# Operands moved to other offsets in on-chip memory, and loads and cuts re-ordered, in a three-layer kernel

## The chip, the cores and the metric

One core of one Trainium2 chip runs the program. The metric is the device time of one execution in microseconds; the median of several runs counts. The profile is of one execution.

## The reference

Three layers follow each other, all in float32; no matrix may lose precision beyond that.

```python
scores = q @ k.T / sqrt(64) - log(448)        # 4 batches, 12 heads, 448 positions, 64 columns
x = sigmoid(scores) @ v                       # rearranged to 1792 tokens x 768
h = maximum(maximum(x @ w1, x @ w2), x @ w3)  # 768 x 768 each
y = h @ w_out1                                # 768 x 768
f = y @ w_in                                  # 768 x 2048
g = maximum(f, 0) + alpha * minimum(f, 0)
out = g @ w_out2                              # 2048 x 768
```

The weights arrive as float64; the kernel reads them as pairs of 32-bit words.

## The kernel before

**Numbers.** Each float32 operand is cut into a high part in float32r (ScalarE, `split_ops.hi`) and a rest (VectorE, `split_ops.lo`); a product is three matmuls, high x high, high x low, low x high (`three`, line 632). The matrices of the layers behind attention are multiplied by a seven-product scheme on 2 x 2 blocks (`unit_ops`, `form_ops`, `product`, `ff3`), so that sums and differences of blocks are made on VectorE before and after.

**Stages.** (1) Attention (line 369): 24 pairs of heads. `load_pair` brings q and k by eight DMAs of 32 partitions each, as runs of 32 floats, on SP's queue, two pairs ahead; `prep_ops` turns and cuts them; `scores` (line 494) makes a chunk of 128 keys at a time, ScalarE's sigmoid writes it into `a` tiles, `av` multiplies it with v. The first pair is loaded in rows and turned by TensorE against an identity (`first_pair`, line 398). (2) `product` (line 748): 9 units of the first weights, then, behind the `c` groups (line 817), 8 units of `w_in`; a unit is 14 products of 9 matmuls. (3) `c_group`: 24 groups of 18 matmuls, h times the fourth matrix. (4) `ff3` (line 937): 42 groups of 24 matmuls, g times the last matrix, with its operands stored to HBM and loaded again (`keep`, `load_g`, `load_w`).

**Order.** TensorE's order is written out by hand. The work of ScalarE ("A") and VectorE ("D"), loads ("L") and DMA issues ("Q") are `Op`s in two lists, `urgent` and `flow`; `advance` (line 168) is called after each piece of TensorE work with the columns that it took, gives both engines that much credit, and emits each op whose predecessors were emitted in an earlier step and whose gate is open. So an op's place in its engine's stream is set by the step in which it is emitted, and an instruction that waits holds all behind it on its engine. `load_half` (line 109) loads a half of a weight block on SP's queue into one of four `wr` buffers; `word_ops` (line 219) turns 64-bit words into float32 and asks for the half four places on. `unit_ops(0)` is started at pair 18 (line 595). `cut_h` for t = 2 and 3 is put into the list in the rounds (1, 1) and (2, 0) of the `c` stage (line 920).

**Memory.** Tiles lie in pools, on the left `const`, `wpool` and `slots_a` (later `slots_l`), on the right `edge`, `apool` (later `slots_c`, `slots_e`). A slot is 448 floats, 7 x 256 bytes, a weight slot 384 floats, 6 x 256 bytes. `bias_s` is 128 bytes wide, and `alpha_sb` and `nalpha` are 64 and 160, and with these every slot, weight slot and attention tile begins at a multiple of 256 bytes. In a matmul the moving operand (448 columns) is an `x`, `y`, `h` or `rf` slot, or q or `a` in attention; the stationary one (128 columns) is a weight slot or `lf`, or k or v. `swap` (line 1210) frees the pool c and opens e in its place, for the high and low parts of g; `turn_left` frees a and opens l.

Of the kernel before, what the change touches and what calls it, by code (L numbers as in the profile page):

```python
# [9 lines left out]
F32 = mybir.dt.float32  # L10
# [6 lines left out]
P = 128  # L17
# [4 lines left out]
def kernel(  # L22
# [43 lines left out]
    pools = {}  # L66
    room = {"a": 76, "c": 24, "e": 24, "l": 36}

    def slot(nm, pool="a", w=TW, dt=F32):
        return pools[pool].tile([P, w], dt, tag="s" + pool, name=nm, bufs=room[pool])  # L70

    def wslot(nm, dt=F32, pool="w"):

# [65 lines left out]
            self.lag = lag  # L139


    free = {"wr": 8, "wl": 4, "wk": 8, "ws": 5, "wf": 4, "rr": 14, "e": 8}
    urgent, flow = [], []
    STEP = 1700
    credit = {"A": 0, "D": 0}
# [73 lines left out]
    def word_ops(z, gate=None):  # L219


        st = {}

        def first():
            st["r"] = wraw.pop(z)
            st["T"] = wslot(f"wt{z}", U32)
            nc.scalar.activation(  # L227
                st["T"].bitcast(F32), st["r"][:, :, 1].bitcast(F32), AF.Abs, scale=2.0**-112
            )
            nc.scalar.activation(st["r"][:, :, 0], st["r"][:, :, 0], AF.Copy, scale=2.0**-29)  # L230

        def whole():
            nc.vector.tensor_scalar(st["T"], st["T"], 3, None, ALU.logical_shift_left)  # L233
            nc.vector.scalar_tensor_tensor(  # L234
                out=st["r"][:, :, 0],
                in0=st["r"][:, :, 1],
                scalar=0x80000000,
                in1=st["r"][:, :, 0],
                op0=ALU.bitwise_and,
                op1=ALU.bitwise_or,  # L240
            )
            nc.vector.tensor_tensor(out=st["T"], in0=st["r"][:, :, 0], in1=st["T"], op=ALU.add)  # L242
            word[z] = st["T"].bitcast(F32)
            load_half(z + 4)

        o = op(
            "A", 2 * HF, first,
            gate=lambda: z in since and tick[0] > since[z] + 3 and (gate is None or gate()),
        )
        return op("D", 3 * HF, whole, o)  # L250

    def split_ops(dst, make, src, w, *deps, seen=lambda x: x, put=lambda x: x, **kw):

# [115 lines left out]
    def attention(apool, ps_s, ps_v):  # L369
# [9 lines left out]
            for c in range(2)  # L379
            for p in (r, r + HK)  # L380
        ]
        raw, prepped, vts, at, pv = {}, {}, {}, {}, {}
# [4 lines left out]

        def load_first():

            kn, qn = (slot(x).rearrange("p (n d) -> p n d", d=32) for x in ("kn", "qn"))  # L390
            for t, src, queue in ((kn, k, nc.sync), (qn, q, nc.scalar)):
                queue.dma_start(
                    out=t.rearrange("p n d -> p (n d)"),
                    in_=src[0, :2].rearrange("j (p n) d -> (j p) (n d)", p=D),
                )
            raw[0] = (qn, kn)

        def first_pair():

            qn, kn = raw.pop(0)  # L400
            for which, t in (("k", kn), ("q", qn)):
                ps = ps_s.tile([P, 2, 512], F32, tag="sc", name=f"turn_{which}")[:, 0, :S]
                rows = t.rearrange("p n d -> p (n d)").rearrange("p (n d) -> p n d", d=D)
                for n in range(S // D):
                    for j in range(2):
                        nc.tensor.matmul(
                            ps[j * D : (j + 1) * D, n * D : (n + 1) * D],
                            rows[:, n],
                            ident[:, j * D : (j + 1) * D],
                            start=(n == 0),  # L410
                            stop=(n == S // D - 1),
                            skip_group_check=True,
                        )
                if which == "k":
                    hi, lo = (x[:, :S] for x in kk[0])
                else:
                    hi, lo = slot("qh0", dt=F32R), slot("ql0", dt=F32R)
                    prepped[0] = (hi, lo)

                seen = ps.rearrange("p (n r) -> p r n", r=D)  # L420
                hi, lo = (x.rearrange("p (r n) -> p r n", r=D) for x in (hi, lo))
                nc.scalar.copy(hi, seen)
                nc.vector.tensor_sub(lo, seen, hi.bitcast(F32))

        def load_v(i, queue):
            b, p = pairs[i]
            vt = apool.tile([P, 2, NCH + 1, D], F32, tag="vt", name=f"vt{i}", bufs=4)
            k0, h0, r0 = (KH, 0, KH) if i % 2 else (0, S - KH, 0)
# [65 lines left out]
        def scores(i, c, sc=None, stop=True):  # L494
# [10 lines left out]
            for z, (kx, qx) in enumerate(((kh, qh), (kl, qh), (kh, ql))):  # L505
# [80 lines left out]
        for i in range(0, n, 2):  # L586
            for z in range(2):
                if i + z + 2 < n:
                    load_pair(i + z + 2)
                if i + z == 8:  # L590
                    for h in range(4):
                        load_half(h)
                    with nc.allow_non_contiguous_dma(reason="a column of slopes per partition"):
                        nc.sync.dma_start(out=alpha_sb, in_=alpha.rearrange("(m p) -> p m", p=P))
                if i + z == 18:
                    unit_ops(0, zu[0])
                ops = prep_ops(i + z + 1)

# [62 lines left out]
    def ff(ps_m, dpool, swap, turn_left):  # L661
# [4 lines left out]
        def prelu(u, g, i, t, src, add=None):  # L666

            f, b = 2 * (u - ND0) + i, 2 * g + t
            s, o = {}, None
            if add is not None:  # L670
                o = op("D", TW, lambda: tensor_op(add, src, add, ALU.add), soon=True)

            def parts():
                x = src if add is None else add
                s["r"], s["n"] = slot(f"r{f}_{b}"), slot(f"n{f}_{b}")
# [15 lines left out]
            (p, o0), (r, o1) = slopes[u, g, 0, 0], slopes[u, g, 1, 1]  # L691

            def sum1():
                s["t"] = slot(f"t1_{u}_{g}")
                tensor_op(s["t"], s["r"], p["r"], ALU.subtract)

            def sum3():
# [8 lines left out]
        def keep(u, g, what, src, o):  # L706
            kp = u - ND0

            def store():
                x = fd[what, g, kp] = dpool.tile(  # L710
                    [P, TW], F32, tag=f"g{len(fd)}", name=f"gd{what[0]}{what[1]}_{g}_{kp}"
                )
                nc.gpsimd.dma_start(out=x, in_=src())  # L713

            stored.append(op("Q", 0, store, o))

        def evict(u, g, i, t, src, other=None):

# [186 lines left out]
        for n, (g, r) in enumerate(quads):  # L905
# [10 lines left out]
            for i in range(2):  # L916
                if g == 0 and r < HK - 1 and i == 0:
                    for h in range(4):
                        conv_ops(NB + 4 * (r + 1) + h)
                if g == 0 and (r, i) in ((1, 1), (2, 0)):  # L920
                    for m in range(KDM - 2):
                        cut_h(m, 1 + r, far[m, 1 + r])
                for t in range(2):
                    c_group(r + HK * i, 2 * g + t)
                    if (n, i, t) == (0, 0, 0):
# [4 lines left out]
            (0, 1), (0, 0), (2, 1), (3, 1), (2, 0), (4, 1), (1, 1), (3, 0), (5, 1), (6, 1),  # L930
        ))
        swap()
        for k in seq[3:]:
            step(ND1 - 1, k, 0)
        run[0](stored)

    def ff3(ps_m, dpool, fd, wd, slopes, seq, turn_left):

# [8 lines left out]
        def load_op(homes, make, src, gate, lag):  # L947
# [3 lines left out]
            def home():  # L951
                return [
                    h for h in homes
                    if free[h] > 0
                    and (h in ("wr", "ws", "wf", "e") or "l" in pools)
                    and (h != "wf" or len(pair) == KP // 2 and free["wr"] == KP)
                ]

# [47 lines left out]
        def left_ops(k, kp):  # L1006
# [183 lines left out]

        return run
# [72 lines left out]
```

## Time and profile before

| | |
|---|---|
| median of 3 runs | 877.12 us |
| lowest, highest | 876.55, 886.61 us |
| the profiled execution | 877.7 us |
| its span, first to last instruction | 875.6 us |
| TensorE (PE) busy | 867.1 us |
| weight loads (PEld) | 747.8 us |
| VectorE (DVE) | 676.2 us |
| ScalarE (ACT) | 527.8 us |

Times of the rows are microseconds from the span's start unless marked ns. PE is the matmul, PEld the weight load that runs beside it; SPq, ACTq and POOLq are DMA issues by those engines. A matmul's own duration in a row includes its way through the array, so that one starts before its predecessor ends: the pace is read from starts. What stands behind `<-` at a row's end is what ended the idle time before it.

### The profile page before, as it was taken

Reading aid. Unit: us, or ns where it says so; the run is one execution under the profiler, and the core shown is the slowest. Engines: PE = TensorE matmul, PEld = TensorE weight load, DVE = VectorE, ACT = ScalarE, POOL = GpSimd, SP = SyncE. Lnnn points to the kernel's source line nnn. Section 1 sums busy time; section 2 is a strip of 40 time slices with the busy share of each in tenths; the row PEclk is TensorE's granted clock in tenths of the full one; section 3 lists DMA queues with packets and bytes.
Section 4 is the critical chain, followed back from the end, with each engine's and each line's share of the span. In section 5 each row is a group of like instructions: output and inputs, shape, how many; then the busy total and the mean of one; then the engine's idle time right before and its main releaser. Section 6 shows DMA issues by size and latency. Waiting matters only on the chain.

```text
span 875.6 us, 13589 instructions
## 1 busy us (share of the span) xinstructions
PE 867.1 (99%) x4604; PEld 747.8 (85%) x4604; DVE 676.2 (77%) x1323; ACT 527.8 (60%) x1034; POOL 146.5 (17%) x249
## 2 busy tenths in 40 slices
PE   9999999999999999999999999999999999999997
PEld 4555557999999999999899999999998999999997
DVE  5888895888889878787687877777766778768851
ACT  5888896755655554666566767667664755443430
POOL 4333320002111201200000122122211011001211
PEclk9999999999999999999999999999999999999999
DMA  8887570547675655632112443354426999445412
GB/s 159 149 181 142 107 170 1 153 127 231 208 203 159 223 146 170 216 91 73 36 53 99 135 148 134 137 178 167 154 97 209 371 335 373 164 151 159 136 49 64
DMA packets 180501, 137.00 MB, mean 156 GB/s; under 512 B 100576, under 2 KB 170336, under 8 KB 180432
## 3 DMA queue, kind: packets, MB, share of 16 engines
q1 hardware_dynamic: 163536, 93.25, 38.5%
q0 software_dynamic: 13952, 42.09, 13.2%
q10 hardware_dynamic: 2944, 0.80, 0.4%
q8 instruction: 36, 0.59, 0.3%
q14 instruction: 33, 0.27, 0.1%
HBM read 102.28 MB, written 33.82 MB: 155 GB/s over the span
## 4 chain that ended last, share of the span: by engine, by line
PE 96%; DVE 1%; ACT 1%; issue 1%; DMA 0%; SPq 0%; DVEq 0%; ACTq 0%
PE u_1X L652 14%; PE u_0X L652 14%; PE eW L652 10%; PE c L652 10%; PE eX L652 10%; PE pav L529 7%; PE u_1W L652 7%; PE u_0W L652 7%; PE sc L508 7%; PE u_1V L652 4%; PE eV L652 3%; PE u_0V L652 3%; DMA kr<-in_k_dram 0%; PE warm L580 0%; ACT r L676 0%
## 5 line engine op out<-in xcount | busy, mean ns | idle before, releaser
L519 ACT ACTIVATE a<-sc,bias_s 128x896 f32<-128x896 f32 x84 | 82.2, 1015 | 13.8 <-PE sc L508 13.8
L529 PE MATMUL pav<-a,vt 128*64 128x448 f32 (+1 forms) x384 | 70.3, 551 | 0.0
L227 ACT ACTIVATE wt<-wr 128x384 f32<-128x384 f32 x112 | 62.1, 555 | 12.4 <-DMA wr<-in_moe_w_dram 5.4
L242 DVE CUSTOM_DVE_ANT_0 wt<-wr,wt 128x768 uint16<-128x768 uint16 x112 | 62.6, 559 | 3.9
L234 DVE SCALAR_TENSOR_TENSOR wr<-wr 128x384 uint32<-128x384 uint32 x112 | 62.0, 554 | 0.9
L230 ACT ACTIVATE wr<-wr 128x384 uint32<-128x384 uint32 x112 | 61.9, 552 | 0.0
L680 DVE SCALAR_TENSOR_TENSOR r<-n,nalpha,r 128x448 f32<-128x448 f32 x64 | 43.3, 683 | 22.4 <-ACT n L677 22.3
L713 POOL DMA_DIRECT2D gd<-r x48 | 26.0, 541 | 201.0 <-DVE r L680 199.2
L529 PEld LDWEIGHTS pav<-a,vt 128*64 128x64 f32 (+1 forms) x384 | 21.0, 135 | 38.5 <-issue 36.8
L430 POOL DMA_DIRECT2D vt<-in_v_dram x46 | 35.3, 769 | 64.0 <-PE pav L529 63.6
L871 POOL DMA_DIRECT2D wd<-wt x32 | 17.5, 546 | 169.5 <-DVE wt L242 149.6
L1108 POOL DMA_DIRECT2D out_dram<-o x28 | 17.6, 635 | 168.3 <-DVE o L1103 168.3
L233 DVE TENSOR_SCALAR wt<-wt 128x384 uint32<-128x384 uint32 x112 | 39.8, 355 | 5.6 <-ACT wt L227 5.6
L508 PE MATMUL sc<-qh,kh 64*128 64x448 f32 x192 | 38.1, 393 | 1.7 <-DVE qh L482 0.9
L780 ACT COPY u<-u_1X 128x448 f32<-128x448 f32 x34 | 18.1, 533 | 33.0 <-PE u_1X L652 33.0
L508 PE MATMUL sc<-ql,kh 64*128 64x448 f32 x192 | 35.4, 365 | 0.0
L508 PEld LDWEIGHTS sc<-qh,kh 64*128 64x128 f32 x192 | 18.0, 184 | 20.2 <-ACT a L519 7.8
L508 PE MATMUL sc<-qh,kl 64*128 64x448 f32 x192 | 35.0, 361 | 0.0
L832 ACT COPY y<-c 128x448 f32<-128x448 f32 x24 | 12.8, 533 | 34.1 <-PE c L652 34.0
L780 ACT COPY u<-u_0X 128x448 f32<-128x448 f32 x34 | 18.1, 534 | 25.0 <-PE u_0X L652 24.4
L276 DVE TENSOR_TENSOR u<-u_0W,u 128x448 f32<-128x448 f32 x28 | 17.4, 623 | 19.3 <-ACT u L780 18.7
L767 ACT COPY u_0V<-u_0X 128x448 f32<-128x448 f32 x17 | 8.8, 518 | 32.7 <-PE u_0X L652 32.7
(836 smaller groups left out, 2882.1 us busy)
## 6 DMA issues: line engine op xcount, KB each, us to landing
gl<-gd SPq DMA_DIRECT2D x79, 224.0 KB, 4.4
wr<-in_moe_w_out_dram SPq DMA_DIRECT2D x44, 384.0 KB, 4.2
wr<-in_moe_w_dram SPq DMA_DIRECT2D x36, 384.0 KB, 3.8
wr<-in_moe_w_in_dram SPq DMA_DIRECT2D x32, 384.0 KB, 3.8
wl<-wd SPq DMA_DIRECT2D x64, 192.0 KB, 4.1
gd<-r POOLq DMA_DIRECT2D x48, 224.0 KB, 2.2
gl_T<-gdT SPq DMA_DIRECT2D x32, 224.0 KB, 5.1
wd<-wt POOLq DMA_DIRECT2D x32, 192.0 KB, 4.0
```

The lines of the kernel that those rows point to most:

```text
L227: nc.scalar.activation(st["T"].bitcast(F32), st["r"][:, :, 1].bitcast(F32), AF.Abs, scale=2.0**-112)
L230: nc.scalar.activation(st["r"][:, :, 0], st["r"][:, :, 0], AF.Copy, scale=2.0**-29)
L233: nc.vector.tensor_scalar(st["T"], st["T"], 3, None, ALU.logical_shift_left)
L234: nc.vector.scalar_tensor_tensor(out=st["r"][:, :, 0], in0=st["r"][:, :, 1], scalar=0x80000000, in1=st["r"][:, :, 0], op0=ALU.bitwise_and, ...
L242: nc.vector.tensor_tensor(out=st["T"], in0=st["r"][:, :, 0], in1=st["T"], op=ALU.add)
L430: queue.dma_start(out=vt[:, j, :NCH], in_=v[b, 2 * p + j, k0 : k0 + NCH * P].rearrange("(c p) d -> p c d", p=P),)
L508: nc.tensor.matmul(sc[:, j, :S], kx[r, c0 : c0 + P], qx[r], start=(start and z == 0), stop=(stop and z == 2),)
L519: nc.scalar.activation(a, sc[:, :, :S], AF.Sigmoid, bias=bias_s, scale=scale)
L529: nc.tensor.matmul(pv[i][j * D : (j + 1) * D, :S], vts[i][r, j, c, :], a[r, j, :], start=start, stop=stop,)
L652: nc.tensor.matmul(ps[:, : rh.shape[-1]], lt, rh, start=(start and z == 0), stop=(stop and z == len(mms) - 1), skip_group_check=True,)
L680: nc.vector.scalar_tensor_tensor(out=s["r"], in0=s["n"], scalar=nalpha[:, f : f + 1], in1=s["r"], op0=ALU.mult, op1=ALU.add,)
L780: nc.scalar.copy(side[g, k], banks[X][:, :TW])
```

## The change

Pads of 48 floats (192 bytes) are put in front of the slots of a and, in l, behind the tag `lf`; pads of 16 floats (64 bytes) stand behind the slots in the pools on the right, whose slots begin 64 bytes lower by that. So moving operands of these pools begin 192 bytes behind a multiple of 256; stationary ones in `wpool`, `apool` and `lf` begin at 0. The first pair's q and k share one attention tile; q is turned first, and k's first 128 columns are turned and cut on their own, with positions left in the order that the turn gives, and v of that pair is loaded to match. The first eight halves of weights ask for the next half in an op of their own; `unit_ops(0)` starts at pair 14; `cut_h` for t = 2 and 3 goes into rounds (1, 0) and (1, 1). Behind `swap` stands one more `advance`; the seven `gl` loads of the last layer's first operand go into `a` slots before `swap` instead of `e` slots behind it; two late results go into `e` slots, which are given back when they are stored; the last operand is put into the list after product 5 instead of at `plan`.

```diff
+    def pad(pool, w):
+        if pool not in padded:
+            padded.add(pool)
+            pools[pool].tile([P, w], F32, tag="pad", name=f"pad_{pool}")
+
     def slot(nm, pool="a", w=TW, dt=F32):
-        return pools[pool].tile([P, w], dt, tag="s" + pool, name=nm, bufs=room[pool])
+        if pool == "a":
+            pad(pool, 48)
+        t = pools[pool].tile([P, w], dt, tag="s" + pool, name=nm, bufs=room[pool])
+        if pool != "a":
+            pad(pool, 16)
+        return t
...
-    free = {"wr": 8, "wl": 4, "wk": 8, "ws": 5, "wf": 4, "rr": 14, "e": 8}
+    free = {"wr": 8, "wl": 4, "wk": 8, "ws": 5, "wf": 4, "rr": 14, "e": 4, "a": 7}
...
-            load_half(z + 4)
+            if z >= 8:
+                load_half(z + 4)
...
-        return op("D", 3 * HF, whole, o)
+        o = op("D", 3 * HF, whole, o)
+        if z < 8:
+            op("Q", 0, lambda: load_half(z + 4), o, lag=1)
+        return o
...
-            kn, qn = (slot(x).rearrange("p (n d) -> p n d", d=32) for x in ("kn", "qn"))
+            t = apool.tile([P, 2, S], F32, tag="a", name="kqn", bufs=2 * NCH + 1)
+            kn, qn = (t[:, x].rearrange("p (n d) -> p n d", d=32) for x in range(2))
...
+            for t, ps, n0, n1 in ((qn, ps_q, 0, S // D), (kn, ps_k0, 0, 2), (kn, ps_k, 2, S // D)):
...
+            nc.scalar.copy(qh, seen)
+            nc.vector.tensor_copy(first_k[0], ps_k0)
+            nc.vector.tensor_sub(first_k[1], ps_k0, first_k[0].bitcast(F32))
+            nc.vector.tensor_sub(ql, seen, qh.bitcast(F32))
+            nc.scalar.copy(kh, ps_k)
+            nc.vector.tensor_sub(kl, ps_k, kh.bitcast(F32))
...
+            if i == 0:
+                n = S // D
+                for j in range(2):
+                    rows = v[b, 2 * p + j].rearrange("(r n) d -> r n d", n=n)
+                    for x in range(2):
+                        queue.dma_start(out=vt[x * D : (x + 1) * D, j, :NCH], in_=rows[:, x : n - 1 : 2])
+                queue.dma_start(
+                    out=vt[:KH, :, NCH],
+                    in_=v[b, 2 * p : 2 * p + 2].rearrange("j (r n) d -> r j n d", n=n)[:, :, n - 1],
+                )
...
+            if (i, c) == (0, 0):
+                kh, kl = first_k
+                three = ((kh, qh), (kl, qh), (kh, ql))
+            elif i == 0:
+                three = ((kh, qh), (kh, ql), (kl, qh))
...
-                if i + z == 18:
+                if i + z == 14:
                     unit_ops(0, zu[0])
...
+            home = lambda: "e" if (u, i, t) == (ND1 - 1, 0, 1) and "e" in pools else "a"
...
+            if u == ND1 - 1 and what in ("T1", "T3"):
+                o.ends.append({"h": "e"})
...
-                if g == 0 and (r, i) in ((1, 1), (2, 0)):
+                if g == 0 and (r, i) in ((1, 0), (1, 1)):
                     for m in range(KDM - 2):
-                        cut_h(m, 1 + r, far[m, 1 + r])
+                        cut_h(m, 2 + i, far[m, 2 + i])
...
         swap()
+        advance(STEP)
         for k in seq[3:]:
             step(ND1 - 1, k, 0)
-        run[0](stored)
+            if k == 5:
+                run[0][0]()
+        run[0][1](stored)
...
+                    and (h != "a" or (U, seq[2], 1) in made)
...
-                ("rr", "e") if n else ("e",),
-                lambda h: slot(nm, "e") if h == "e" else tile_l("rr", nm, TW, 14),
-                lambda: fd[key], lambda: ("l" if n else "e") in pools and key in fd,
-                8 if n else 1 if kp < 3 else 2,
+                ("rr", "e") if n else ("a",),
+                lambda h: tile_l("rr", nm, TW, 14) if h == "rr" else slot(nm, h),
+                lambda: fd[key], lambda: (not n or "l" in pools) and key in fd,
+                8 if n else 1,
...
+                if (k, kp, x) == (1, 0, "h"):
+                    return lf[k, kp][x]
...
-                return ((U, seq[kp - 4], 0) if kp > 3 else (U - 1, 6, 1)) in made
+                return ((U, seq[kp - 3], 0) if kp > 3 else (U - 1, 6, 1)) in made
...
+        def last_right():
+            right_ops(0, KP - 1, soon=True)
+
         def plan():
-            right_ops(0, KP - 1, soon=True)
...
+                        lf[1, 0]["h"] = tile_l("lf", "lf1_0h", HF, 2 * KP, F32R)
+                        pad("l", 48)
```

## Rows read from the trace of the kernel before

**Rows 1.** The page: busy us (share of the span) and instructions of each engine.

```profile
PE 867.1 (99%) x4604; PEld 747.8 (85%) x4604; DVE 676.2 (77%) x1323; ACT 527.8 (60%) x1034; POOL 146.5 (17%) x249
```

**Rows 2.** Stretches: us, busy PE, PEld, DVE, ACT, POOL (instructions), PE clock, DMA share, GB/s.

```profile
100.00:150.00 50.00, 48.98 (x327) 28.59 (x324) 40.22 (x81) 40.78 (x67) 9.09 (x13) 1.00 0.37 84
300.00:350.00 50.00, 50.00 (x249) 46.36 (x248) 39.95 (x82) 26.37 (x57) 6.49 (x12) 1.00 0.57 170
850.00:876.00 26.00, 21.06 (x104) 19.18 (x103) 3.25 (x5) 0.00 (x0) 2.50 (x4) 0.98 0.23 54
```

**Rows 3.** Pieces of the chain that ended last: start, us, engine, tile, instructions.

```profile
375.28 44.65 PE c L652 x216
...
486.18 3.65 PE u_1X L652 x18
...
725.14 58.37 PE eW L652 x288
```

**Rows 4.** Middle of a unit, timeline of PE and PEld; its weight loads in the groups.

```profile
300.05 0.37 PE L652 MATMUL u_1V<-x_1h,f_1l 128*128 128x448 f32 x1
300.05 0.19 PEld L652 LDWEIGHTS u_1V<-x_1l,f_1h 128*128 128x128 f32 x1
...
300.25 0.36 PE L652 MATMUL u_1V<-x_1l,f_1h 128*128 128x448 f32 x1
...
L652 PEld LDWEIGHTS u_0V<-x_1h,f_1h 128*128 128x128 f32 x27 | 5.1, 188 | 0.4
```

**Rows 5.** Attention: timeline of two paired loads of pav; the loads of sc in the groups.

```profile
52.27 0.14 PEld L529 LDWEIGHTS pav<-a,vt 128*64 128x64 f32 x2 [0.23 <-issue]
52.64 0.14 PEld L529 LDWEIGHTS pav<-a,vt 128*64 128x64 f32 x2 [0.23 <-issue]
...
L508 PEld LDWEIGHTS sc<-qh,kh 64*128 64x128 f32 x192 | 18.0, 184 | 20.2 <-ACT a L519 7.8 <-issue 4.2 <-ACT x_4h L256 2.8
```

**Rows 6.** The first 8 us, timeline of all engines.

```profile
1.27 0.96 ACTq L430 DMA_DIRECT2D vt<-in_v_dram  x2
...
4.06 1.21 PE L406 MATMUL turn_k<-ident,kn 128*64 128x64 f32 x28
...
5.09 1.00 PE L406 MATMUL turn_q<-ident,qn 128*64 128x64 f32 x28
5.31 0.53 ACT L422 CAST kh<-turn_k 128x448 fp32r<-128x448 f32 x1 [2.61 <-PE turn_k L406]
...
6.69 0.62 DVE L423 TENSOR_TENSOR ql<-turn_q,qh 128x448 fp32r<-128x448 f32 x1 [0.19 <-ACT qh L422]
6.71 0.47 PE L508 MATMUL sc<-qh,kh 64*128 64x448 f32 x2 [0.62 <-ACT qh L422]
...
7.68 0.36 PE L508 MATMUL sc<-qh,kh 64*128 64x448 f32 x2
```

**Rows 7.** End of attention, timelines of SP's queue, DVE and PE.

```profile
110.12 0.39 SPq L115 DMA_DIRECT2D wr<-in_moe_w_dram  x1
...
121.97 0.65 DVE L466 STREAM_TRANSPOSE kt<-kr 128x448 f32<-128x448 f32 x1 [1.02 <-DMA kr<-in_k_dram]
...
126.80 0.47 PE L508 MATMUL sc<-qh,kh 64*128 64x448 f32 x2 [0.91 <-DVE qh L482]
```

**Rows 8.** Two stretches of PE (us, PE busy, clock, DMA); SP's queue; a wait at 640:675.

```profile
419.74:423.99 4.25, 4.06 (x19) 1.00 0.00 0
664.76:671.47 6.71, 5.97 (x25) 1.00 0.42 153
...
644.90 19.37 SPq L963 DMA_DIRECT2D gl<-gd  x9
...
PEld eX L652 <- DVE rf_0l L260: 0.6, 1, 0.6
```

**Rows 9.** Attention's middle, a stretch as in rows 2; the page's loads of k.

```profile
50.00:100.00 50.00, 50.00 (x370) 27.72 (x368) 39.83 (x78) 41.04 (x57) 20.82 (x30) 1.00 0.81 156
...
kr<-in_k_dram SPq DMA_DIRECT2D x92, 56.0 KB, 2.6
```

More of the change, by code (lines that the diff above doesn't have):

```diff
@@ L67 @@
     room = {"a": 76, "c": 24, "e": 24, "l": 36}
-    def slot(nm, pool="a", w=TW, dt=F32):
-        return pools[pool].tile([P, w], dt, tag="s" + pool, name=nm, bufs=room[pool])
+    padded = set()
+    def pad(pool, w):
+        if pool not in padded:
+            padded.add(pool)
+            pools[pool].tile([P, w], F32, tag="pad", name=f"pad_{pool}")
+    def slot(nm, pool="a", w=TW, dt=F32):
+        if pool == "a":
[4 more added lines that the diff above has]
+        return t
     def wslot(nm, dt=F32, pool="w"):
@@ L381, in attention @@
         ]
-        raw, prepped, vts, at, pv = {}, {}, {}, {}, {}
+        raw, prepped, vts, at, pv, first_k = {}, {}, {}, {}, {}, []
         kk = [
@@ L400, in first_pair @@
             qn, kn = raw.pop(0)
-            for which, t in (("k", kn), ("q", qn)):
-                ps = ps_s.tile([P, 2, 512], F32, tag="sc", name=f"turn_{which}")[:, 0, :S]
+            ps_q = ps_s.tile([P, 2, 512], F32, tag="sc", name="turn_q")[:, 0, :S]
+            ps_k0 = ps_v.tile([P, 512], F32, tag="pv", name="turn_k0")[:, :P]
+            ps_k = ps_s.tile([P, 2, 512], F32, tag="sc", name="turn_k")[:, 0, : S - P]
+            for t, ps, n0, n1 in ((qn, ps_q, 0, S // D), (kn, ps_k0, 0, 2), (kn, ps_k, 2, S // D)):
@@ L403, in first_pair @@
                 rows = t.rearrange("p n d -> p (n d)").rearrange("p (n d) -> p n d", d=D)
-                for n in range(S // D):
+                for n in range(n0, n1):
                     for j in range(2):
                         nc.tensor.matmul(
-                            ps[j * D : (j + 1) * D, n * D : (n + 1) * D],
+                            ps[j * D : (j + 1) * D, (n - n0) * D : (n - n0 + 1) * D],
                             rows[:, n],
                             ident[:, j * D : (j + 1) * D],
-                            start=(n == 0),
-                            stop=(n == S // D - 1),
+                            start=(n == n0),
+                            stop=(n == n1 - 1),
@@ L412, in first_pair @@
                             skip_group_check=True,
                         )
[L414 to L423, printed above, removed]
+            prepped[0] = slot("qh0", dt=F32R), slot("ql0", dt=F32R)
@@ new lines, in first_pair @@
+            seen = ps_q.rearrange("p (n r) -> p r n", r=D)
+            qh, ql = (x.rearrange("p (r n) -> p r n", r=D) for x in prepped[0])
+            kh, kl = (x[:, P:S] for x in kk[0])
+            first_k.extend(slot(f"k{x}00", dt=F32R)[:, :P] for x in "hl")
+            nc.scalar.copy(qh, seen)
[3 more added lines that the diff above has]
+            nc.scalar.copy(kh, ps_k)
@@ L427, in load_v @@
             vt = apool.tile([P, 2, NCH + 1, D], F32, tag="vt", name=f"vt{i}", bufs=4)
+            if i == 0:
[8 more added lines that the diff above has]
+                )
+                vts[i] = vt
+                return
             k0, h0, r0 = (KH, 0, KH) if i % 2 else (0, S - KH, 0)
@@ L504, in scores @@
                 sc = ps_s.tile([P, 2, 512], F32, tag="sc", name=f"sc{i}_{c}")
-            for z, (kx, qx) in enumerate(((kh, qh), (kl, qh), (kh, ql))):
+            three = ((kh, qh), (kl, qh), (kh, ql))
+            if (i, c) == (0, 0):
+                kh, kl = first_k
+                three = ((kh, qh), (kl, qh), (kh, ql))
+            elif i == 0:
+                three = ((kh, qh), (kh, ql), (kl, qh))
+            for z, (kx, qx) in enumerate(three):
                 for j in range(2):
@@ L674, in parts @@
                 x = src if add is None else add
-                s["r"], s["n"] = slot(f"r{f}_{b}"), slot(f"n{f}_{b}")
+                s["r"], s["n"] = slot(f"r{f}_{b}", home()), slot(f"n{f}_{b}")
                 nc.scalar.activation(s["r"], x, AF.Relu)
@@ L693, in sum1 @@
             def sum1():
-                s["t"] = slot(f"t1_{u}_{g}")
+                s["t"] = slot(f"t1_{u}_{g}", home())
                 tensor_op(s["t"], s["r"], p["r"], ALU.subtract)
@@ L713, in store @@
                 nc.gpsimd.dma_start(out=x, in_=src())
-            stored.append(op("Q", 0, store, o))
+            o = op("Q", 0, store, o)
+            stored.append(o)
+            if u == ND1 - 1 and what in ("T1", "T3"):
+                o.ends.append({"h": "e"})
         def evict(u, g, i, t, src, other=None):
@@ L954, in home @@
                     if free[h] > 0
-                    and (h in ("wr", "ws", "wf", "e") or "l" in pools)
+                    and (h in ("wr", "ws", "wf", "e", "a") or "l" in pools)
+                    and (h != "a" or (U, seq[2], 1) in made)
                     and (h != "wf" or len(pair) == KP // 2 and free["wr"] == KP)
@@ L1189, in run @@
             drain()
-        return run
+        return last_right, run
     with tc.manual_schedule():
```

## The prediction

> **What bounds the kernel now.** I read the busy shares first, then PE by stretches, then the chain in order of time, because an engine that is busy for 99% of the span [rows 1] can still be run at a poor pace, and only starts of single instructions tell that. The reader is to see two things. First, PE is hardly ever idle: in the middle of the run whole stretches of 50 us show 50.00 us of PE, and what is missing lies in few places, 1.02 us where attention ends and some 5 us behind the last matmul [rows 2]. So edits that move loads and cuts about can win only the little that is missing. Second, the pace: the chain's pieces give 58.37 us for 288 matmuls, 202.7 ns each, in the last product, and 202.8 ns in the middle one; one stretch, the `c` groups, runs at 44.65/216 = 206.7 ns [rows 3]. The granted clock there is 1.00, the 2.4 GHz level [rows 2], so it isn't the clock.
>
> What sets 202.7 ns? A weight load starts as its predecessor's matmul starts (both at 300.05) and takes 188 ns; the next matmul starts at 300.25 [rows 4]. So load plus some 12 to 15 ns of handing over is the whole period. Where the loaded block is half as wide (`pav`, 64 columns), the load takes 0.14 us and the parallel pair of matmuls follows at 0.377 us, 188.5 ns a matmul [rows 5]: there the load ends long before the stream does, and the period is shorter by 14 ns a matmul. I read this as: outside attention the period is the chain of weight loads, not the stream of the moving operand.
>
> The Trainium skill (TensorE: Matmul & The Clock Gate, Back-to-back issue gap) puts the isolated gap at N/2.4 + 2.5 ns, an estimate of 189 ns for 448 columns; the rows show 202.7, so the rule's term is not the one that binds here. By the rule 14 ns a matmul would be there to win; by the row they are won only if the load gets shorter.
>
> **The change part by part.** The sum is made against the profiled execution's own 877.7 us (875.6 of span and 2.1 around it), 0.6 above the 877.12 median of the runs shown.
>
> *The pads.* They issue no instruction. They move the moving operands of all 3,582 full-width matmuls (17 units x 14 products x 9, 24 `c` groups x 18, 42 `e` groups x 24) from 0 to 192 bytes behind a multiple of 256; stationary operands stay at 0, but for the `c` weights that live in `a` slots. No matmul of the trace has another offset, so their price isn't shown, and I bound it. Below: every matmul falls to the 188.5 ns of `pav` [rows 5], 14.2 x 3,582 = -50.9 us. Above: every matmul goes at the `c` stretch's 206.7 ns [rows 3], 4.0 x 3,582 = +14.3 us. I take 0, nearest to the reading that the loads of stationary blocks, which do not move, are the chain: the load takes 188 ns wherever its matmul's operand lies.
>
> *The first pair* (`first_pair`, `load_v`). Before: k is turned from 4.06, q from 5.09, `kh` is cut at 5.31, `qh` after it, and the first score starts at 6.71, the second chunk at 7.68, held up by `ql` (6.69 to 7.31) [rows 6]. After: q is turned first, so `qh` is cut at 5.31; the 8 + 20 records of k follow, and the first 128 columns are cut on DVE by 5.9, so `sc` starts behind the turns, at 6.1. `ql` ends near 6.6 instead of 7.31, the rest of k is cut on ACT by 6.7, and the second chunk starts at about 6.8: 0.9 us earlier, of which I take 0.8 (next late is the sigmoid, which sets the score banks free). The two more loads of v on ACT's queue take half a microsecond each, by the 0.96 us of two, from 1.27 [rows 6]; `qh` waits until 5.31 in any case, so they are hidden; without that cover they would cost 1.0. Bounds: 0 and -1.0.
>
> *Weights earlier* (`unit_ops(0)` at pair 14, `load_half` as an op of its own one step later). Before, SP stands at a weight load until DVE has emptied its buffer (110.12), and k and q of the next pairs queue behind; DVE then waits for `kr` (1.02 us before 121.97) and PE for `qh` (0.91 us before 126.80) [rows 7]. Four such loads now meet four earlier pairs, each queued a step later on SP. A wait is still behind each, so I take half of the 1.02 us [rows 2], -0.5; bounds -1.0 and +1.0 (it happens once more).
>
> *The `c` stage* (`cut_h` for t = 2, 3 half a round earlier). The group at 419.74 takes 4.25 us for 18 matmuls, 18 x 0.2067 = 3.72 at its own pace, so its wait for the late cuts of h costs 0.5 [rows 8]. The cuts go to steps with free ACT and DVE: -0.5; bounds -0.5 and 0. The pace of 206.7 ends at this wait; without it, it could last longer, and that is a rival below.
>
> *The last product's start* (gl loads into `a` slots before `swap`, one more `advance`, `last_right` after k = 5, T1 and T3 into `e`). SP takes 19.37 us over nine `gl` issues, since the `e` slots they want are still read under their old name. The first group has 24 matmuls in 6.71 us, against 24 x 0.2027 = 4.86: 1.85 us lost in four waits like that for `rf_0l` [rows 8]. Seven loads now have a home of their own; 14 cuts and the last one fit into the four products in front. I take -1.8; bounds -1.85 and 0. What is late next would be the slots of the later `gl`, which start with 4 `e` homes in place of 8 and get four back with the T stores.
>
> Sum: -0.8 - 0.5 - 0.5 - 1.8 = -3.6, so 874.1 for an execution like the profiled one, and 873.5 on the scale of the median.
>
> **The rivals.**
>
> *A: the pace falls.* If the moving stream and the weight load, which start together [rows 4], hinder each other by both beginning at 0, the shift frees some of the 14.2 ns. Half of it is 7.1 x 3,582 = 25 us: 848. For it: load and stream do start within a hundredth of a microsecond, and half-width loads show the shorter period. Against it: the load's 188 ns are the same in every group, and 184 ns for the half-height blocks of `sc` [rows 5].
>
> *B: the pace rises,* by the pads or because no wait ends the 206.7 ns phase any more: 873.5 + 14.3 = 888. For it: that phase follows no operand and lasts 54 us. Against it: the pieces before and after it are at 202.7 [rows 3].
>
> *C: attention becomes bound by DMA (the other side).* The transposing loads bring rows of 32 floats, 128 bytes, which at 0 never cross a multiple of 256 and at 192 cross every second time. 92 such loads of 56 KB each for k, as many for q; the DMA engines are at 0.81 already [rows 9]. If a crossing row costs a second piece, k and q cost up to 1.5 times; at a share of 0.81 x 1.5 = 1.22 the 110 us of attention stretch by 24: 898. It decides once the loads grow by 1/0.81 = 1.23. Against it: k and q are not all of the 0.81.
>
> The Trainium skill (DMA: Bandwidth & Descriptors, How a descriptor splits into AXI transactions) speaks for C: a piece must begin at a 256-byte boundary, and one that doesn't start there is split and pays for the bytes in front. No row here shows a load at another offset.
>
> *D: the edits don't do what they say:* waits move to the next late load, at the end of attention or among the later `gl` (the DMA share is high there too), and what the start wins they lose: 877.
>
> **How the numbers follow.** Forecast 0.55, with a range of its own of 870 to 877; A 0.22; B 0.11; C 0.06; D 0.06. The range reaches down to the middle of A, 848, which leaves out half of it (0.11), and up to B's 890, which leaves out C and a little of B (0.08). Two per cent, about what a measurement of this kernel can tell from no change, is 17.5 us: faster is below 859.6, which takes nine tenths of A, 0.20. Slower is above 894.7: C and 0.02 of B, 0.08. The rest, 0.72, is within.
>
> **What would show it.** Right: the chain's pieces after still at 202 to 203 ns a matmul, loads at 188; `sc` starting near 6.1; 100 to 150 with PE near 49.5; the first `eX` group in 4.9 us. Wrong: a period that has moved by more than 2 ns in `u` or `e`, with the load's start or length moved with it (A, B); PE waiting for `qh` or `kr` over and over between 20 and 110, with the DMA share at 1 (C). The forecast as a whole is wrong if the period per matmul is not 202.7.

## The result, and the profile after

The changed kernel takes 872.04 us (median; 871.82 to 872.61), 0.9897 of the kernel before, with a 95% interval of [0.9866, 0.9928]. In that comparison the kernel before spread from 876.55 to 886.61 with a median of 880.38, which flatters the ratio. A later comparison gave 872.53 against 877.23, 0.9946 [0.993, 0.9961], a ratio that leaves out one execution of the kernel before at 4441.93 us; I take that one, 4.7 us. Both lie within 2%. The profiled execution took 872.05 us, with a span of 870.2; it is 5.65 us shorter than the one profiled before, 0.95 more than the 4.7.

The page's busy shares and the stretches of the kernel after (columns as in [rows 1] and [rows 2]):

```profile
PE 862.4 (99%) x4604; PEld 746.3 (86%) x4604; DVE 677.4 (78%) x1325; ACT 527.4 (61%) x1034; POOL 146.6 (17%) x249
```

```profile
10.00:20.00 10.00, 8.65 (x66) 4.78 (x64) 6.33 (x12) 6.88 (x9) 5.50 (x9) 1.00 0.92 169
...
50.00:100.00 50.00, 49.89 (x366) 27.03 (x363) 42.90 (x85) 44.22 (x66) 20.26 (x29) 1.00 0.84 165
100.00:150.00 50.00, 50.00 (x338) 30.05 (x335) 41.40 (x83) 40.44 (x63) 9.76 (x14) 1.00 0.47 83
300.00:350.00 50.00, 50.00 (x249) 46.36 (x248) 38.98 (x81) 25.38 (x55) 7.00 (x13) 1.00 0.60 172
...
661.60:668.50 6.90, 6.90 (x36) 6.40 (x35) 6.78 (x13) 5.10 (x11) 2.29 (x5) 1.00 0.74 224
```

The holes of [rows 2] and [rows 8] are closed: 100 to 150 has 50.00 us of PE (48.98 before), and the last product's first 6.90 us hold no gap. A new hole stands at the start: 8.65 of 10 us between 10 and 20.

Pieces of the chain that ended last (start, us, engine, tile, instructions), to be held against [rows 3]:

```profile
374.03 83.77 PE c L695 x414
...
661.64 29.12 PE eX L695 x144
...
719.88 58.24 PE eW L695 x288
```

A last-product matmul takes 58.24/288 = 202.2 ns (202.7 before), one of the `c` stage 83.77/414 = 202.3. The 206.7 ns stretch of before is gone. All `c` groups but the first form one piece: no wait divides them any more.

The same place in a unit as [rows 4] on the timeline, and its loads in the groups:

```profile
300.30 0.37 PE L695 MATMUL u_1V<-x_1h,f_1l 128*128 128x448 f32 x1
...
300.30 0.19 PEld L695 LDWEIGHTS u_1V<-x_1l,f_1h 128*128 128x128 f32 x1
...
300.51 0.36 PE L695 MATMUL u_1V<-x_1l,f_1h 128*128 128x448 f32 x1
```

```profile
L695 PEld LDWEIGHTS u_0V<-x_1h,f_1h 128*128 128x128 f32 x27 | 5.1, 187 | 0.5
```

Load and matmul still start together. The mean of all 3,582 recorded loads of a full block went from 187.9 to 187.5 ns, by nearly as much as the period. So these two traces alone don't tell a shorter load from a shorter gap behind it; `e3` below does, with loads of 187.5 ns too and a period of 200.0.

The start of the kernel after, and three marks further on, from the timeline:

```profile
1.21 3.64 SPq L486 DMA_DIRECT2D kr<-in_k_dram  x4
1.26 1.38 ACTq L458 DMA_DIRECT2D vt<-in_v_dram  x2
...
4.41 1.03 PE L430 MATMUL turn_q<-ident,kqn 128*64 128x64 f32 x28 [0.44 <-DMA kqn<-in_q_dram]
...
5.30 2.15 SPq L486 DMA_DIRECT2D qr<-in_q_dram  x4
6.22 0.47 PE L551 MATMUL sc<-qh,kh 64*128 64x448 f32 x2
7.22 0.37 PE L551 MATMUL sc<-qh,kh 64*128 64x448 f32 x2
...
15.90 0.47 PE L551 MATMUL sc<-qh,kh 64*128 64x448 f32 x2 [1.35 <-DVE qh L519]
...
140.64 0.47 PE L695 MATMUL u_0X<-x_0h,f_0l 128*128 128x448 f32 x1
...
865.12 0.36 PE L695 MATMUL eW<-rf_7h,lf_7h 128*128 128x448 f32 x1
```

The same marks of the kernel before (k's and q's loads of the second pair; the third pair's first scores; first `u`; last matmul):

```profile
1.21 3.04 SPq L449 DMA_DIRECT2D kr<-in_k_dram  x4
4.29 2.05 SPq L449 DMA_DIRECT2D qr<-in_q_dram  x4
...
15.03 0.47 PE L508 MATMUL sc<-qh,kh 64*128 64x448 f32 x2
...
141.26 0.47 PE L652 MATMUL u_0X<-x_0h,f_0l 128*128 128x448 f32 x1
...
870.70 0.37 PE L652 MATMUL eW<-rf_7h,lf_7h 128*128 128x448 f32 x1
```

How early the first scores come depends on the clock too. While `turn_q` and `turn_k` run, pairs of matmuls start 107 ns apart until the trace's record of the granted clock begins, at 1.00, and 58 ns apart from then on. It begins at 4.49 before and at 4.39 here, so the two starts can be set against each other to some 0.2 us. In the runs below it begins anywhere between 4.35 and 9.89; the time ahead of it has no record, and prints as 1.00.

The ledger by these marks and by `eX` (664.76 before [rows 8], 661.64 after):

| stretch | change, us | of it |
|---|---|---|
| to the first scores | -0.5 | 6.71 to 6.22 |
| first scores to third pair's | +1.4 | 8.32 to 9.68 |
| on to the first `u` | -1.5 | 126.23 to 124.74; the waits of [rows 7] gone |
| `u` and `c` stages | -2.5 | pads 0.45 ns x 2,574 = 1.2; the `c` wait 0.5; the 206.7 stretch some 1 |
| last product | -2.5 | the waits of [rows 8] 1.85; pads 0.45 ns x 1,008 = 0.5 |

Together -5.6, the difference of 870.70 and 865.12 in the two profiled executions. The rest of this document separates pads from re-ordering and finds what sets 202.2.

### The profile page after: what moved, and what is told of

Read it like the earlier page. It is cut to its first block, busy times and chain, and to the rows that moved or that the text cites. A ratio compares the mean times of both kernels' runs of the same rounds, so it can differ in the third digit from the quotient of the medians.

```text
span 870.2 us, 13603 instructions
## 1 busy us (share of the span) xinstructions
PE 862.4 (99%) x4604; PEld 746.3 (86%) x4604; DVE 677.4 (78%) x1325; ACT 527.4 (61%) x1034; POOL 146.6 (17%) x249
## 4 chain that ended last, share of the span: by engine, by line
PE 98%; DMA 1%; SPq 1%; DVE 0%; issue 0%; DVEq 0%
PE u_0X L695 14%; PE u_1X L695 14%; PE c L695 10%; PE eW L695 10%; PE eX L695 10%; PE pav L572 8%; PE u_0W L695 7%; PE u_1W L695 7%; PE sc L551 7%; PE u_0V L695 4%; PE u_1V L695 4%; PE eV L695 3%; SPq L486 1%; DMA kr<-in_k_dram 0%; DMA qr<-in_q_dram 0%
```

## The experiments

The kernels before of these comparisons had medians of 876.93 (`e1` to `e4`), 877.28 (`e5` to `e8`) and 877.23 (`f1` to `f4`). Each diff is against the changed kernel unless it says otherwise. "Difference" is the start of the moving operand less that of the stationary one, modulo 256 bytes.

**Re-ordering alone** (`e1_no_pads`): difference 0.

```diff
     def pad(pool, w):
-        if pool not in padded:
-            padded.add(pool)
-            pools[pool].tile([P, w], F32, tag="pad", name=f"pad_{pool}")
+        return
```

> The changed kernel without its pads: every operand begins at 0 behind a multiple of 256 again, all else as changed. Theory P (the offset between moving and stationary operands decides whether the chain of weight loads can fall into the 206.7 ns pace, and the pads hold it off): the pace outside attention is 202.7 ns at best, 0.45 above the 202.2 of the changed kernel, which is 3,582 x 0.45 = 1.6 us, and some stretches at 206.7 come back: 874 to 880 us, with several us between the runs. Rival S (the pace of 206.7 came from the waits that the re-ordering took away, the pads do nothing but the 0.45): 873.6 us, runs within 1 us, no stretch at 206.7.

Measured: 873.39 (873.01 to 873.88), 0.9962 [0.995, 0.9975]. Its chain:

```profile
720.86 58.37 PE eW L693 x288
```

Its timeline: q's loads of the second pair, the first and the third pair's scores, the first `u`:

```profile
5.16 1.96 SPq L484 DMA_DIRECT2D qr<-in_q_dram  x4
6.83 0.47 PE L549 MATMUL sc<-qh,kh 64*128 64x448 f32 x2
...
15.44 0.47 PE L549 MATMUL sc<-qh,kh 64*128 64x448 f32 x2 [0.27 <-DVE qh L517]
...
140.41 0.47 PE L693 MATMUL u_0X<-x_0h,f_0l 128*128 128x448 f32 x1
```

Its stretch from 50 to 100:

```profile
50.00:100.00 50.00, 49.89 (x366) 27.13 (x364) 42.93 (x86) 44.24 (x66) 20.57 (x29) 1.00 0.77 159
```

That is what rival S expected, 873.6 and no stretch at 206.7. The pace is 58.37/288 = 202.7, as before. All re-ordering together is worth 876.93 - 873.39 = 3.5 us. SP's second batch goes out at 5.16, not 4.29: that push belongs to the re-ordering, not to the pads. The first scores are at 6.83 and not at 6.22 because the clock's record begins at 6.25 here. The third pair's scores still wait 0.27 us for q, so their 15.44 is set by the loads. The same stretch of attention has a DMA share of 0.77 with rows at 0 and 0.84 with rows at 192; but the kernel before has 0.81 at 0, and the second run of the change (`f1`) 0.80 at 192, so the difference isn't clear of what changes from one execution to the next.

**Pads alone** (`e2_pads_only`): the kernel before with `pad`, its two calls in `slot` (48 for a, 16 for the others) and the one behind `lf`. Of the diff against the kernel before, the part in `slot`:

```diff
...
-        return pools[pool].tile([P, w], dt, tag="s" + pool, name=nm, bufs=room[pool])
+        if pool == "a":
+            pad(pool, 48)
+        t = pools[pool].tile([P, w], dt, tag="s" + pool, name=nm, bufs=room[pool])
+        if pool != "a":
+            pad(pool, 16)
+        return t
...
```

> The kernel before with the pads alone. Theory P: 202.2 ns throughout, also in the c groups (270 x 4.4 = 1.2 us less there, 1.6 us less elsewhere), all waits of the kernel before stay: 877.7 - 2.8 = 875 us, runs within 1 us of each other. Rival S: as the kernel before, 876.5 to 886.6, a stretch at 206.7 behind one of its waits.

Measured: 875.8 (874.57 to 876.66), 0.9987 [0.9978, 0.9996]. Its chain, and then its timeline at the first scores:

```profile
375.34 43.72 PE c L665 x216
...
723.65 58.24 PE eW L665 x288
```

```profile
7.37 0.47 PE L521 MATMUL sc<-qh,kh 64*128 64x448 f32 x2 [0.62 <-ACT qh L435]
```

The pads alone bring 202.2 ns. They win 1.1 us, less than the 1.6 of the pace, and stay 0.8 above the 875 expected; the runs spread over 2.1 us. The profiled execution has its first scores 0.66 us later than before (7.37 against 6.71 [rows 6]), but the clock's record begins at 5.87 in it, against 4.49, so this isn't shown to be the pads' doing. The `c` stage goes at 43.72/216 = 202.4 although its late cuts are still waited for, so the end of the 206.7 stretch doesn't need the re-ordering.

**Another offset** (`e3_moving_64`): moving operands at 64 in place of 192.

```diff
-            pad(pool, 48)
+            pad(pool, 16)
...
-            pad(pool, 16)
+            pad(pool, 48)
...
-                        pad("l", 48)
+                        pad("l", 16)
```

> The changed kernel with moving operands 64 in place of 192 bytes behind a multiple of 256, stationary ones at 0 as before. If any offset between the two will do: 872 us and 202.2 ns, runs within 1 us. If it has to be 192: like the kernel without pads, 874 to 880 us and 202.7 ns or stretches at 206.7.

Measured: 864.76 (864.53 to 864.9), 0.9863 [0.985, 0.9877]. Its chain:

```profile
371.78 83.13 PE c L695 x414
...
714.11 57.60 PE eW L695 x288
```

57.60/288 = 200.0 ns, 7.3 us less than the change as made. Neither expectation held: the offset matters, and 192 isn't the best.

**Both operands at 192** (`e4_all_at_192`): difference 0 again, with nothing at 0 outside attention.

```diff
-        if pool == "a":
-            pad(pool, 48)
...
-    bias_s = const.tile([P, 32], F32, name="bias_s")[:, :1]
+    bias_s = const.tile([P, 80], F32, name="bias_s")[:, :1]
...
-                        pad("l", 48)
```

> The changed kernel with the weight slots and lf also 192 bytes behind a multiple of 256, so that moving and stationary operands outside attention have no offset between them but both differ from 0. If the offset between the two counts: like the kernel without pads, 874 to 880 us, 202.7 or 206.7 ns. If the place of the moving operand by itself counts: 872 us and 202.2 ns. If the place of the stationary one counts, the load of 188 ns changes, and the period with it by the same number of ns.

Measured: 878.4 (877.54 to 878.83), 1.0017 [1.0008, 1.0026]. Its chain:

```profile
370.53 1.86 PE u_0W L693 x9
372.39 1.82 PE u_1X L693 x9
...
726.25 58.37 PE eW L693 x288
```

202.7 ns in the last product, as with both at 0; but the first 230 us of `u` ran at 1.86/9 = 206.7 and fell to 202.7 at 372.39. Two steady periods exist at difference 0, as in [rows 3], and neither is tied to a tile. That an absolute place away from 0 helps is out.

**The mirror** (`e6_stationary_192`): moving operands at 0, stationary ones at 192; the difference is -192, which is 64.

```diff
         if pool == "a":
-            pad(pool, 48)
-        t = pools[pool].tile([P, w], dt, tag="s" + pool, name=nm, bufs=room[pool])
-        if pool != "a":
             pad(pool, 16)
+        t = pools[pool].tile([P, w], dt, tag="s" + pool, name=nm, bufs=room[pool])
...
-    bias_s = const.tile([P, 32], F32, name="bias_s")[:, :1]
+    bias_s = const.tile([P, 80], F32, name="bias_s")[:, :1]
...
-                        pad("l", 48)
+                        pad("l", 16)
```

> The changed kernel with the stationary operands outside attention at 192 and the moving ones at 0: the difference is 64 again, taken modulo 256. Theory R (the difference counts, modulo 256): 200.0 ns as with moving at 64 and stationary at 0; and as q and k rows fall on whole 128s, about 1 us less at the start: 863.5 us. Rival M (the moving operand's own place counts): 202.7 ns as without pads, 873.4 us. Under both the wait before the third pair's scores is 0.6 us and not 1.7.

Measured: 864.89 (864.73 to 865.7), 0.9862 [0.9847, 0.9876]. Its chain:

```profile
371.77 83.65 PE c L693 x414
...
714.63 57.60 PE eW L693 x288
```

200.0 ns again, as in `e3`, with every absolute place another and only the difference alike. The time is 1.4 us above theory R's 863.5. Its `c` stage is longer than that of `e3` (83.65 against 83.13), and the single groups tell why. Eight of the 24 `c` groups take their weights from `a` slots and so have difference 0 in both kernels; the other groups have 64. In `e3` the eight go at 202.4 to 202.7 ns, here one at 202.7 and seven at 206.3 to 206.7; the other sixteen go at 200.0 in both, but for the first behind a change (up to 200.7). So the pace changes within one stage, from group to group, with the difference, and difference 0 shows its two periods again.

**More differences**: 128 (`e5_moving_128`, pads of 32, 32 and 32 floats), 96 (`e8_moving_96`, 24, 40 and 24) and 32 (`f2_moving_32`, 8, 56 and 8). The diff of the last:

```diff
-            pad(pool, 48)
+            pad(pool, 8)
...
-            pad(pool, 16)
+            pad(pool, 56)
...
-                        pad("l", 48)
+                        pad("l", 8)
```

> The changed kernel with moving operands at 128, stationary at 0. Shown so far at 0, 64, 192: 202.7 (or 206.7), 200.0, 202.2 ns. If any offset that is a whole 64 and not 0 shortens the period: 200 to 202.2 ns, 864 to 872 us. If 64 alone is good: 202.2 ns or more, 872 us or more. As 128-byte rows of q and k fall on whole 128s again, the wait before the third pair's scores shrinks from the 1.7 us of the changed kernel to the 0.63 us of the kernel without pads under either.

> The changed kernel with moving operands at 96. If what counts is in which block of 64 bytes the operand begins: the period is that of 64, 200.0 ns, 864.8 us. If finer steps count: a value between those of 64 and 128, other than 200.0.

> The changed kernel with moving operands at 32, stationary at 0. Differences so far: 0: 202.7 or 206.7, 64: 200.0, 96: 205.3, 128: 204.0, 192: 202.2 ns. If the period depended on whole blocks of 64: 202.7 or 206.7, as at 0. If a start in the middle of 64 costs by itself (as 96 against 64 and 128): 205 ns or more, 883 us.

Measured: 128: 878.54 (878.04 to 880.16), 1.0017 [1.0008, 1.0026]. 96: 883.77 (883.26 to 886.44), 1.0073 [1.0056, 1.009]. 32: 888.9 (888.26 to 890.51), 1.0126 [1.0105, 1.0148]. The piece of the last product of each, in this order, the loads of `f2`, and the stretch from 10 to 20 of `e8` and of `f2`:

```profile
725.64 58.76 PE eW L695 x288
```

```profile
732.03 59.14 PE eW L695 x288
```

```profile
735.13 59.52 PE eW L695 x288
```

```profile
L695 PEld LDWEIGHTS u_0V<-x_1h,f_1h 128*128 128x128 f32 x27 | 5.1, 188 | 0.5
```

```profile
10.00:20.00 10.00, 7.54 (x52) 4.87 (x50) 6.63 (x12) 5.42 (x7) 5.16 (x9) 0.90 0.90 168
```

```profile
10.00:20.00 10.00, 8.38 (x62) 4.67 (x58) 6.75 (x12) 6.60 (x8) 5.13 (x9) 0.91 0.91 173
```

| difference | ns a matmul | runs |
|---|---|---|
| 0 | 202.7, in stretches 206.7 | before, `e1`, `e4` |
| 32 | 206.7 | `f2` |
| 64 | 200.0 | `e3`, `e6`, `f3`, `f4` |
| 96 | 205.3 | `e8` |
| 128 | 204.0 | `e5` |
| 192 | 202.2 | after, `e2` |

6.7 ns times 3,582 matmuls is 24 us, which is the distance of `f2` and `e3` (24.1). The recorded load is 187 to 188 ns in all of them. At 128 the period is longer, as it was to be if 64 alone is good. At 96 neither expectation held, as 205.3 isn't between 200.0 and 204.0. At 32 the 206.7 fits both, the dependence on whole blocks of 64 and the price of a start in the middle of 64; but 96 lies in the block of 64 and is 5.3 ns off it, so whole blocks are out.

In the profiled executions of `e8` (886.44 us) and `f2` (890.51) PE waited 2.46 and 1.62 us for the third pair, and the granted clock fell to 0.50, the 1.2 GHz level, from 18.0 to 21.4 and from 18.2 to 21.6: hence the 0.90 and 0.91 above. The paces of the table are from stretches at 1.00.

The expectation for 128 also held that the wait at the third pair would go, since rows of 128 bytes cross no multiple of 256 there; the profile of `e5` still has it:

```profile
16.38 0.47 PE L551 MATMUL sc<-qh,kh 64*128 64x448 f32 x2 [1.15 <-DVE qh L519]
```

So that wait comes without crossing rows too.

**Who pushes SP's loads** (`e7_v_by_pool`): the first pair's five loads of v go to GpSimd's queue.

```diff
-        load_v(0, nc.scalar)
+        load_v(0, nc.gpsimd)
```

> The changed kernel with the five loads of the first v issued by GpSimd's queue in place of ScalarE's. If these loads are what pushes back SP's loads of q and k (SP's second pair of loads begins at 5.30 in place of 4.29 before): SP is back at 4.3, the 1.7 us wait before the third pair's scores is at most 0.7, 871.0 us. If the rows of q and k that cross a multiple of 256 are the whole of it: the wait stays above 1.5 us, 872 us.

Measured: 872.01 (871.48 to 873.65), 0.9944 [0.9929, 0.9959]: no gain. The start of the profiled execution (873.65 us):

```profile
3.23 2.32 SPq L486 DMA_DIRECT2D qr<-in_q_dram  x4
4.75 1.76 PE L430 MATMUL turn_q<-ident,kqn 128*64 128x64 f32 x28 [0.79 <-DMA kqn<-in_q_dram]
...
7.94 0.74 PE L551 MATMUL sc<-qh,kh 64*128 64x448 f32 x2
```

SP's second batch goes out at 3.23 instead of 5.30, and its first four issues took 1.98 us instead of 3.64: v's loads on ACT's queue do hold SP's back. PE is busy for 9.93 us of the 10 from 10 to 20, without a wait for the third pair. But that needn't be the edit's gain: the first scores are at 7.94 here, and in `e6`, with v on ACT's queue and first scores at 7.39, PE is busy for 9.92 us of the same 10. The first q now lands later, and the turns took 1.76 us instead of 1.03, since the clock's record begins at 9.89 and not at 4.39; that is also why the `sc` of 7.94 took 0.74 us in place of 0.47. Over the runs turns took 1.0 to 1.8 us, by where in them the record begins. So what this edit is worth at an equal clock stays open.

**The change once more** (`f1_changed_again`), as it is.

> The changed kernel once more, beside a steady kernel before on one chip, to set against the kernel without pads (0.9962) and the kernel before with the pads alone (0.9987). If the pads give the 0.45 ns of the period and no more, 1.6 us: ratio 0.994 to 0.9945, 872 us, the product of those two ratios (0.9949) within 0.1 per cent. If the first comparison's 0.9897 was the pads' too: below 0.991.

Measured: 872.53 (872.23 to 874.19), 0.9946 [0.993, 0.9961]; 58.24 us for the piece of 288. Against `e1` the pads win 0.9 (1.4 by the first comparison's 872.04), less than the pace's 1.6. With pads the third pair's scores start later, at 15.90 in the first profile and 16.31 in this one, against 15.44.

**Pads at 64 on the kernel before** (`f3_before_moving_64`): as `e2`, with 16, 48 and 16 floats. Of the diff against the kernel before, the three calls:

```diff
...
+            pad(pool, 16)
...
+            pad(pool, 48)
...
+                        pad("l", 16)
...
```

> The kernel before with pads alone that put its moving operands at 64. If the period follows from the difference alone, whatever the order of the work: 200.0 ns in u and e, 2.67 x 3,582 = 9.6 us and the c stretch's phase (1.1 us) less than the kernel before: 866.5 us, ratio 0.988. If the gain needs the changed order: 0.995 or more.

Measured: 868.51 (868.26 to 869.41), 0.9898 [0.9882, 0.9915], 2 us above what was expected. Its timeline, at the first turn and the first scores, explains most of it:

```profile
4.55 1.76 PE L419 MATMUL turn_k<-ident,kn 128*64 128x64 f32 x28 [0.58 <-DMA kn<-in_k_dram]
...
8.18 0.48 PE L521 MATMUL sc<-qh,kh 64*128 64x448 f32 x2 [0.62 <-ACT qh L435]
```

First scores at 8.18, 1.47 us later than before [rows 6]: the clock's record begins at 7.13 here, against 4.49. Another 0.4 is the eight `c` groups of difference 0, at 202.7 as in `e3`. One edit, a few pads, still wins 8.7 us without any re-ordering.

**All pairs at 64** (`f4_all_pairs_at_64`): `e6`, with the `c` weights that live in `a` slots put 192 bytes into them. The diff is against `e6`:

```diff
-            return slot(nm, pool, HF, dt)
+            return slot(nm, pool, TW, dt)[:, 48 : 48 + HF]
```

> As the kernel with stationary operands at 192 and moving ones at 0, with the c weights that live in a slots also put 192 bytes in, so that every pair outside attention differs by 64. The 144 matmuls of c0 and c3, 206.7 and 205.2 ns there, go at 200.0: 0.8 us, and what follows at a longer pace with them: 863.9 us. If these did not depend on the difference: 864.9.

Measured: 863.94 (863.39 to 864.4), 0.9844 [0.9826, 0.9862], the best here: 13.3 us under the kernel before and 8.6 under the change. Its chain:

```profile
371.16 82.80 PE c L693 x414
...
713.16 57.60 PE eW L693 x288
```

The `c` stage too is now at 82.80/414 = 200.0 ns; its 0.85 us against `e6` are the 0.95 of the medians. That the difference of each pair of operands sets its pace was foretold by the expectation to 0.1 us.

## Why the prediction was right, and where

The verdict (within 2%), the time (872.0 and 872.5 for 873.5) and the likeliest case's own range (870 to 877) were right. The total was right partly because terms of both signs were missed.

*Right: the re-ordering as a sum, in part by luck.* -3.6 foretold, -3.5 measured by `e1`, in which a first pair that lost instead of won stands against weights that won more than foretold and some 1 us of the 206.7 stretch, which was not in the sum. *Right: where time is missing.* The three holes read from [rows 7] and [rows 8] closed. The `c` wait gave its 0.5 and the last product its 1.85, both as taken.

*Mis-sized: weights earlier.* "A wait is still behind each, so I take half of the 1.02 us": the stretch from the third pair to the first `u` became 1.5 us shorter, 1.3 in `e1` (126.23 to 124.97). SP no longer stands long at a weight load that has loads of q and k behind it. Its waits for a buffer at such weight loads, from 60 to 141 us, before and then after (us in total, times, longest; a longer wait in each, 29.6 and 26.6 us, starts when the last k and q are out and holds none of them back):

```profile
SPq L115 <- DVE wt L242: 11.6, 2, 10.6
```

```profile
SPq L128 <- DVE wt L255: 5.8, 3, 2.6
```

*Failed: "they are hidden".* The first pair was given -0.8. Its own part came near: `sc` at 6.22 for a foretold 6.1, the second chunk at 7.22 for 6.8 (7.68 before). But the cover named for the additional loads of v was ACT's wait for `qh`; the wrong queue was watched. SP's `kr` loads, beside which v's were issued, took 3.64 us for four instead of 3.04, and SP's next batch left 1.01 us later, about the 1.0 that the prediction priced for a lost cover. PE then waited 1.35 us for the third pair, whose scores start 0.87 us later than before: the -0.8 became +0.9. `e1` gives 0.41 of this to the re-ordering (15.44 for 15.03). The rest comes with the pads, and the 0 that was taken for them left it out: with v's loads on ACT's queue in the changed order, PE waits 1.15 to 2.46 us for the third pair in all seven profiled executions with q and k off 0 (after, `e3`, `e4`, `e5`, `e8`, `f1`, `f2`), and at most 0.27 in the three with q and k at 0 (`e1`, `e6`, `f4`). Why isn't shown.

*Failed: "I take 0" for the pads.* The step was "the load takes 188 ns wherever its matmul's operand lies". That sentence is true to half a ns: the means of all runs lie between 187.5 and 188.0. What was wrong is to conclude from it that the period stays: beyond its load a period holds another 12 to 19 ns, and those depend on the difference of the two operands' starts. At 192 this was worth 0.45 ns, 1.6 us in all; by the prediction's own test ("wrong if the period per matmul is not 202.7") its reading failed, by little. At 64 the same reading would have missed 9.6 us, at 32 14.3 the other way. The bounds, -50.9 and +14.3, held all of them.

*Rivals.* A came nearest: where moving stream and load begin does count, with 1.6 us at a sixteenth of its 25. But the reason given for it, that both begin at 0, is refuted by `e4`, where both begin at 192 and nothing is won. B's price is what `f2` showed: 206.7 throughout, 888.9 for its 888. That the pace would stay up once the `c` wait is gone was not seen: `e1` has neither the wait nor the 206.7. Whether before's other runs have that stretch isn't shown. Rival C, on the other side, didn't come: PE is busy for 49.89 of 50 us between 50 and 100, and the DMA share there was 0.84, and 0.80 in `f1`, against 0.81 before, where C needed 1.23 times as much.

The Trainium skill (DMA: Bandwidth & Descriptors, How a descriptor splits into AXI transactions) has each AXI transaction start at a multiple of 256 bytes, so that a descriptor which starts elsewhere also fetches, and pays for, the bytes in front. It speaks of what is fetched; here the side that moved is where the rows land. Shares of 0.84 and 0.80 at 192, and of 0.81 and 0.77 (`e1`) at 0, show no clear price, and none as large as C's.

## What to carry to other kernels

Where PE is busy all the time and its pace is load plus a few ns, try where the two operands of a matmul begin relative to each other: a pad of 64 bytes cost nothing to write and won 1% of a whole kernel (`f3`), while 32 and 96 cost 1.6 and 1.1% against the same kernel without pads (`f2` and `e8` against `e1`). Measure several offsets, since the first one tried (192) shows a sixth of what the best gives. And when small loads are added beside a critical queue, look for who else issues at that moment: the engine that issues them is not the only one that pays. Before you compare the first microseconds of two executions, see where in each the clock rose.

## What the runs showed of the hardware that was not expected

The period of a float32r matmul of 448 columns with a 128 x 128 load depends on the difference of the operands' start addresses modulo 256 bytes, from 200.0 ns at 64 to 206.7 at 32, at a granted clock of 1.00 and with the recorded load at 187 to 188 ns. 32, 96 and 128 are worse than the 202.7 of 0; 160 and 224 were not tried. What in the memory or in TensorE makes it isn't shown by any run. At difference 0 there are two steady periods, 202.7 and 206.7, of which one can last 230 us (`e4`) and then give way to the other; what decides between them isn't shown.

Where the record of the granted clock begins, and with it the change from 107 to 58 ns in the turns, moves from 4.35 to 9.89 us over fourteen executions, though PE runs the same matmuls ahead of the turns in all; the first scores lie between 6.22 and 8.18.

The Trainium skill (SBUF — State Buffer, A bandwidth-pool intuition that's wrong) gives the weight loads a read port of their own beside the moving operand's. By that no difference would count; `f2` and `e3`, 24 us apart in the same program, show that it does here, and the measurement decides.
